# FNet mixing and a gelu MLP in one fp32 kernel: small products and a lane swap later in their step, and the next batch's first-stage groups in other steps

## The chip, the cores and the metric

The kernel runs on 1 core of one Trainium2 chip. The metric is the device time in microseconds (us), the median of several runs. Three runs of the kernel before took 1855.01, 1855.89 and 1854.38 us: median 1855.01 us.

## The reference

```python
def _attn_ref(x):                       # x: (8, 3008, 256) float32
    X = np.fft.fft(x, axis=1)
    X = np.fft.fft(X, axis=2)
    return X.real.astype(np.float32)

def _moe_ref(x, w_in, w_out):           # (24064, 256), (256, 2048), (2048, 256), float32
    h = x @ w_in
    g = h * (1.0 / (1.0 + np.exp(-1.702 * h)))
    return (g @ w_out).astype(np.float32)

def reference(x, moe_w_in, moe_w_out):  # the real part of the 2-d transform, then the MLP
    a = _attn_ref(x)
    return _moe_ref(a.reshape(8 * 3008, 256), moe_w_in, moe_w_out)
```

## The kernel before

**Work.** A transform over 3008 = 47 x 64 points is done in two stages per batch: `fold1` (GpSimd) adds and subtracts mirrored rows of the input tile `xt` in place, `mix1` (TensorE, 47-row products) is the first stage, `spill` and `fill` carry its result through DRAM into the tile `t4`, `rotate` mends one column, and `stage2` (TensorE, products on 64 rows and 32 columns) is the second stage, whose result `pq` is already folded over the model dimension. The first matrix of the MLP has the last transform folded into it (`wcs`), so the hidden layer is `wcs` times `pq`; its second half comes from the first by symmetry (`backward` subtracts the hidden value from twice its even part, reversed in order). The second matrix product is done by a Strassen-like scheme: 7 large products of which the kernel keeps 3 (`product`), and whose other 4 are split again into 7 small ones each (`small_products`, key k = 1 to 7).

**Steps.** The hidden layer is walked in 384 steps: 8 batches of 48 steps, each batch 3 blocks of 16, each block two halves (`hh`) of NP = 8 steps. This document writes t for the number of a step and m for t modulo 48. Steps with m = 8 to 15 are 226 wide, all others 256. Eight steps that share one output are a group; it ends where m is 7, 15, 23, 31, 39 or 47. In the trace, batch 2 (t = 96 to 143) runs from 495.31 to 720.15 us.

**What a step t issues**, in the order of the loop from line 989, from t = 8 on:

- TensorE: `begin(t, 1)` (second half of the hidden values, 8 records `x<-pq,wcs`), then `product` of step t-3 (LAG = 3; 12 records `o<-big,wo`), `begin(t+1)` (8 records), and the small products. Those of an odd step t' come in two parts: `one` = (1, 2, 4, 7) in step t'+3, which is even, and `other` = (5, 6, 3) in step t'+4, which is odd. One k is 8 records of 128 columns. `cut` says how many of the three products of `product` stand ahead of `begin(t+1)`.
- ScalarE: `forward(t)` (L607, gelu out of PSUM), `doubled(t+1)` (L604, twice the even part), `activate_back(t)` (L614), `middle(t+2)` (two L592, which start the PSUM bank of step t+2).
- VectorE: `backward(t)` (L565), `sums(t-1)` in even steps (L629, L630), `deeper` (three L651 in odd steps, one in even steps).
- GpSimd: `sums(t)` (L622, L623).

Each engine works its own list in order. The hidden values of a step lie in PSUM bank b0 or b1, by the parity of t. `middle(t+2)` can write that bank only when `backward(t)` has read it, `begin(t+2)` adds to what `middle(t+2)` wrote, and `begin(t+1, 1)` may go on only when `doubled(t+1)` has copied the even part out.

**The end of a group** with last step g: ScalarE copies out of PSUM in step g+3 (`combine`, L754 and L756), VectorE adds the small results in step g+4 (`combine_small`, four L786), ScalarE exchanges lanes in step g+5 (`swap`, three copies L794 to L796), VectorE adds again in step g+5 (`combine_last`, L768 and L804), and turns and stores the two halves in steps g+6 and g+7 (`turn_last`, L737).

**The next batch beside it.** A table `extra` says at the end of which step a piece of the next batch is issued. For batch 0 the folds run in steps 11 to 26 and `mix1` in 16, 20, 25, 28; for batches 1 to 6 the folds run at m = 6 to 21 and `mix1` at m = 12, 15, 19, 23. `stage2` stands at m = 8, 24 and 40. A step that holds `mix1` or `stage2` is called special: these take the step's own bank (b0 or b1) and b2 for their result, so `middle(t+2)` is put off into the next step, ahead of its `forward`. The step after a special one is called `after`: there `cut` is 3, and one k of the small products stands ahead of `begin(t+1)`. The folds issue per part: part 0 is L225 and L227, part 1 is L230 and L231; the first part of a batch has L218, L219 and L220 ahead of it.

Of the kernel before, what the change touches and what calls it, by code (L numbers as in the profile page):

```python
# [43 lines left out]
LAG = 3  # L44
# [68 lines left out]
def kernel(ctx: ExitStack, tc, x, w_in, w_out, tab1, tab2, out):  # L113
    nc = tc.nc
# [470 lines left out]
    def middle(t):  # L585

        b, blk, hh, p = steps[t]
        n = width(t)
        x = xb[t] = bank("x", f"b{t % 2}")
        for i in range(2):  # L590
            f = 2 * p + i
            nc.scalar.activation(x[:, i * 256:i * 256 + n], nbt[b, blk][:, hh * 256:hh * 256 + n], ACTF.Copy,  # L592
                                 scale=af1[:, f:f + 1])
# [194 lines left out]
    def swap(t):  # L788

        if not group_end(t):  # L790
            return
        n = width(t)
        one, two_, kept = (free(big[lo:lo + 64], RES + at, [512, 2], [1, n]) for lo, at in ((64, 0), (0, 256), (64, 1024)))
        nc.scalar.copy(kept, two_)  # L794
        nc.scalar.copy(two_, one)
        nc.scalar.copy(one, kept)  # L796
# [136 lines left out]
    def at(t, fn, *args):  # L933
        extra.setdefault(t, []).append((fn, args))
# [22 lines left out]
        at(7 + i, small_weights, i)  # L957
    for b in range(B):
        t0 = b * NBLK * NF
        late = 0 if b else 5  # L960
        if b + 2 < B:
            for k in range(3):
                at(t0 + 11 + k, paced, t0 + 11 + k)
                at(t0 + 11 + k, turn, b + 2, k)
        if b + 1 < B:
            for c in range(NCH):
                for part in range(2):
                    at(t0 + 6 + 2 * c + part + late, fold1, b + 1, c, part, nc.gpsimd)
                if c % 2:
                    k = t0 + 9 + 2 * c + late + (c == (5 if late else 1))  # L970
                    at(k, mix1, b + 1, c // 2)
                    for half in range(2):
                        at(k + 1, spill, b + 1, half, c // 2)
            for blk in range(NBLK):
                at(t0 + 27 + blk + late, paced, t0 + 27 + blk + late)
                at(t0 + 27 + blk + late, fill, b + 1, 4 * blk, 4 * blk + 4)
            if b + 2 < B:
                for k in range(4):
                    at(t0 + 31 + 2 * k + late, paced, t0 + 31 + 2 * k + late)
                    at(t0 + 31 + 2 * k + late, load_x, b + 2, k)  # L980
            at(t0 + 36 + 3 * (late > 0), rotate, b + 1)
        for blk in range(NBLK):
            nxt = (b, blk + 1) if blk + 1 < NBLK else (b + 1, 0)
            if nxt[0] < B:
                at(t0 + blk * NF + 8, stage2, *nxt)
                at(t0 + blk * NF + 9, nyquist_out, *nxt)
                at(t0 + blk * NF + 10, nyquist, *nxt)

    for t in range(n + LAG):
        if t < NP:  # L990
            if t == NP - 3:
                spare[:] = [tag for tag in spare if tag[0] == "o"] + ["b2"]
            if t == NP - 1:
                middle(NP)
            hidden(t)
            if t == NP - 1:
                begin(NP)
                no_row(1024)
            if t == 0:
                squares(in2, nc.scalar)  # L1000
                nyquist(0, 0)
                low_up(in2)
                low_down(in2)
            if t in rows_at:
                first_row(rows_at[t])
            if t >= LAG and t != LAG + 1:
                product(t - LAG, 0, None)
            if t == LAG:
                product(1, 0, None)
            if t == 5:  # L1010
                bounds(("out", 2))
            if t == 6:
                low_down(("out", 3))
            if t:
                activate(t - 1)
            if t == 3:
                bounds(("in", 3))
            if t == 5:
                bounds(("out", 3), False)
            if t in early:  # L1020
                fold_w(early[t])
            rows(t)
            if t == NP - 1:
                doubled(NP)
                middle(NP + 1)
        else:
            after, special = (any(fn in (mix1, stage2) for fn, _ in extra.get(k, ())) for k in (t - 1, t))
            if t < n:
                begin(t, 1)
            if t == NP:  # L1030
                activate(t - 1)
            if after and t + 1 < n:
                middle(t + 1)
            if t < n:
                forward(t)
            while waiting:
                m, ps = waiting.pop()
                mixed(m, 1, ps)
            opening = (t - LAG) % NP == 0 and t >= NP + LAG
            one, other = (t - LAG, (1, 2, 4, 7)), (t - LAG - 1, (5, 6, 3))  # L1040
            if opening:
                small_products(*other)
            cut = 0 if opening and not after else 3 if after else 2
            product(t - LAG, 0, cut)
            if after:
                small_products(one[0], one[1][:1])
                small_products(other[0], () if opening else other[1][:1])
            if t + 1 < n:
                begin(t + 1)
            if not opening:  # L1050
                small_products(other[0], other[1][after:])
            product(t - LAG, cut, 6 if t - LAG == last else None)
            small_products(one[0], one[1][after:])
            swap(t - LAG - 2)
            if t < n:
                backward(t)
            if t + 1 < n:
                doubled(t + 1)
            if t < n:
                activate_back(t)  # L1060
                sums(t, nc.gpsimd)
            if t + 2 < n and not special:
                middle(t + 2)
            combine_small(t - LAG - 1)
            if t - LAG == last:
                product(last, 6, None)
            sums(t - 1, nc.vector)
            deeper(t - 2, 0)
            deeper(t - 3, 1)
        if t == NP:  # L1070
            psu.close()
            low = ctx.enter_context(tc.tile_pool(name="low", bufs=1, space=PS))
            pot["low"] = low.tile([128, 3 * 512], F32, tag="low", name="low")
        if t >= LAG:
            combine(t - LAG)
            combine_last(t - LAG - 2)
            turn_last(t - LAG - 3, 0)
            turn_last(t - LAG - 4, 1)
        if t >= NP:
            spare[:] = [f"b{t % 2}"] * special + ["b2"]  # L1080
        for fn, args in extra.get(t, ()):
            fn(*args)
# [28 lines left out]
```

## Time and profile before

| | |
|---|---|
| median of the runs | 1855.01 us |
| the profiled execution | 1854.86 us |
| its span | 1853.1 us |
| TensorE busy | 1836.6 us (99%) |
| VectorE busy | 1520.9 us (82%) |
| ScalarE busy | 1150.5 us (62%) |
| GpSimd busy | 975.2 us (53%) |
| one batch (t = 96 to 143) | 224.84 us |

In the rows of the timeline a group of records of one kind has the start of its first record and the time to the end of its last. TensorE's matmuls overlap, so what counts there is the time from one start to the next: 8 records of 256 columns take 0.86 to 0.87 us from start to start, 8 of 128 columns 0.43 to 0.44 us.

### The profile page before, as it was taken

How to read it: one execution, taken by the hardware profiler on the slowest of the kernel's cores; microseconds unless marked ns; L12 is line 12 of the kernel's file. 1: busy time of each engine (PE TensorE's matmuls, PEld its weight loads, DVE VectorE, ACT ScalarE, POOL GpSimd, SP SyncE). 2: the span in 40 equal slices, each digit the busy share in tenths (PEclk: the TensorE clock that was granted, in tenths of full speed). 3: DMA queues.
4: the chain of work that ended last, by engine and by line, in shares of the span. 5: the costliest groups of instructions: out<-in, count | busy, mean ns of one | idle time of the engine just before them, and what ended most of it. 6: DMA issues, size and time to landing. Idle time of an engine off the chain costs nothing.

```text
span 1853.1 us, 56093 instructions
## 1 busy us (share of the span) xinstructions
PE 1836.6 (99%) x23722; PEld 1401.3 (76%) x23722; DVE 1520.9 (82%) x2222; ACT 1150.5 (62%) x2241; POOL 975.2 (53%) x1053
## 2 busy tenths in 40 slices
PE   8999999999999999999999999999999999999998
PEld 4677777777777777777777777777777777778776
DVE  6988778887798778987789878888888888878874
ACT  5666656665666666666566666666665666656663
POOL 4776446744368434773348643485445754444442
PEclk9999999999999999999999999999999999999999
DMA  8721340215012240223302132121411111100111
GB/s 280 181 61 34 85 67 19 72 52 99 19 46 48 73 81 13 52 50 90 57 13 67 43 86 52 19 75 35 103 31 23 37 46 36 31 19 13 23 19 24
DMA packets 149707, 105.31 MB, mean 57 GB/s; under 512 B 106057, under 2 KB 130665, under 8 KB 148896
## 3 DMA queue, kind: packets, MB, share of 16 engines
q1 hardware_dynamic: 146624, 99.68, 23.6%
q8 instruction: 187, 3.06, 0.7%
q10 hardware_dynamic: 2832, 2.05, 0.5%
q14 instruction: 64, 0.52, 0.1%
HBM read 64.41 MB, written 48.05 MB: 61 GB/s over the span
## 4 chain that ended last, share of the span: by engine, by line
PE 80%; DVE 9%; POOL 4%; ACT 2%; DMA 2%; issue 2%; SPq 0%; DVEq 0%; ACTq 0%; POOLq 0%
PE x L184 29%; PE o L184 22%; PE low L685 21%; PE o L685 3%; DVE big L651 3%; PE ps L255 2%; DVE big L786 2%; DVE big L565 1%; PE ps L365 1%; POOL xt L227 1%; DVE big L629 1%; POOL big L623 1%; DMA xt<-in_x_dram 1%; ACT big L607 1%; DMA Td<-big 1%
## 5 line engine op out<-in xcount | busy, mean ns | idle before, releaser
L622 POOL TENSOR_TENSOR big<-big 128x256 f32<-128x256 f32 (+1 forms) x376 | 353.0, 939 | 825.1 <-ACT big L614 691.4
L184 PE MATMUL x<-pq,wcs 128*64 128x256 f32 (+1 forms) x6016 | 768.8, 376 | 2.0 <-ACT g L604 1.4
L651 DVE TENSOR_TENSOR big<-big 128x512 f32<-128x512 f32 (+1 forms) x736 | 623.1, 861 | 23.4 <-PE low L685 4.7
L184 PE MATMUL o<-big,wo 128*64 128x256 f32 (+1 forms) x4800 | 620.8, 375 | 0.1
L184 PEld LDWEIGHTS x<-pq,wcs 128*64 128x64 f32 x6016 | 412.3, 137 | 186.0 <-issue 15.0
L184 PEld LDWEIGHTS o<-big,wo 128*64 128x64 f32 x4800 | 341.6, 137 | 148.0 <-DVE big L629 0.5
L604 ACT ACTIVATE g<-x 128x512 f32<-128x512 f32 (+1 forms) x376 | 221.6, 589 | 366.3 <-PE x L184 365.0
L565 DVE TENSOR_TENSOR big<-g,x 128x512 f32<-128x512 f32 (+2 forms) x440 | 254.1, 589 | 209.4 <-ACT big L607 209.0
L592 ACT ACTIVATE x<-nb,af 128x256 f32<-128x256 f32 (+1 forms) x752 | 352.9, 469 | 79.7 <-DVE pq L371 63.6
L685 PE MATMUL low<-big 128*64 128x128 f32 (+1 forms) x5888 | 382.8, 270 | 0.0
L685 PEld LDWEIGHTS low<-big 128*64 128x64 f32 x5888 | 337.5, 137 | 29.2
L623 POOL TENSOR_TENSOR big<-big 128x256 f32<-128x256 f32 (+1 forms) x376 | 352.6, 938 | 0.0
L607 ACT ACTIVATE big<-x 128x512 f32<-128x512 f32 (+1 forms) x376 | 219.2, 583 | 127.5 <-PE x L184 121.3
L614 ACT ACTIVATE big<-big 128x512 f32<-128x512 f32 (+1 forms) x376 | 231.9, 617 | 46.0 <-DVE big L565 44.0
L685 PE MATMUL low<-big,wo 128*64 128x128 f32 (+1 forms) x2944 | 220.4, 271 | 0.1
L685 PEld LDWEIGHTS low<-big,wo 128*64 128x64 f32 x2944 | 171.3, 137 | 4.2 <-DVE big L651 1.4
L630 DVE TENSOR_TENSOR big<-big 128x512 f32<-128x512 f32 (+1 forms) x188 | 160.8, 855 | 6.5
L629 DVE TENSOR_TENSOR big<-big 128x512 f32<-128x512 f32 (+1 forms) x188 | 137.3, 730 | 5.3 <-POOL big L622 5.3
L786 DVE TENSOR_TENSOR big<-big,low 128x512 f32<-128x512 f32 (+3 forms) x184 | 109.0, 609 | 3.5
L685 PEld LDWEIGHTS o<-big,wo 128*64 128x64 f32 x1472 | 92.2, 137 | 25.0
L685 PE MATMUL o<-big,wo 128*64 128x128 f32 (+1 forms) x1472 | 110.0, 270 | 0.0
L227 POOL TENSOR_TENSOR xt<-xt 111x510 f32<-111x510 f32 x56 | 86.0, 1535 | 4.4
(95 smaller groups left out, 966.2 us busy)
## 6 DMA issues: line engine op xcount, KB each, us to landing
out_dram<-os SPq DMA_DIRECT2D x284, 64.0 KB
t<-Td SPq DMA_DIRECT2D x22, 512.0 KB
Td<-xt SPq DMA_DIRECT2D x56, 192.0 KB
xt<-in_x_dram SPq DMA_DIRECT2D x14, 512.0 KB
xt<-Xr SPq DMA_DIRECT2D x14, 512.0 KB
nb<-Nd SPq DMA_DIRECT2D x23, 256.0 KB
out_dram<-os SPq DMA_DIRECT2D x96, 56.0 KB
Xr<-in_x_dram SPq DMA_DIRECT2D x7, 752.0 KB
```

Source lines behind the costliest of these rows:

```text
L184: nc.tensor.matmul(out[c0:c0 + 64], lhsT=lhs[:, c0:c0 + 64], rhs=rhs, skip_group_check=True, **how)
L565: nc.vector.tensor_tensor(free(out, at + m - 1, [by, 2], [RUN, blocks], [-1, m]), *ins, op=op)
L592: nc.scalar.activation(x[:, i * 256:i * 256 + n], nbt[b, blk][:, hh * 256:hh * 256 + n], ACTF.Copy, scale=af1[:, f:f + 1])
L604: nc.scalar.activation(two(g[:], n), two(xb[t][:], n), ACTF.Copy, scale=2.0)
L607: nc.scalar.activation(front(t), two(xb[t][:], width(t)), ACTF.Gelu_apprx_sigmoid)
L614: nc.scalar.activation(back(t), back(t), ACTF.Gelu_apprx_sigmoid)
L622: eng.tensor_tensor(right(t, S1, n), left(t, A21, n), right(t, A22, n), op=ALU.add)
L623: eng.tensor_tensor(left(t, S3, n), left(t, A11, n), left(t, A21, n), op=ALU.subtract)
L629: eng.tensor_tensor(s2, s1, a11, op=ALU.subtract)
L630: eng.tensor_tensor(s4, a12, s2, op=ALU.subtract)
L651: nc.vector.tensor_tensor(out, i0, i1, op=how)
L685: nc.tensor.matmul(o, lhsT=lhs, rhs=rhs, start=first_in, stop=(p == NP - 2), skip_group_check=True)
```

## The change

Four things change.

1. In a step after a special one no small products stand ahead of `begin(t+1)` any more: all of `other` follows `begin(t+1)`, as it does in every other step, and all of `one` ends the step. `cut` stays 3 there.
2. `swap` is issued after `middle(t+2)`, at the end of the step's ScalarE work. Before, it was issued ahead of `doubled(t+1)`.
3. `combine_last` and both `turn_last` come one step later (g+6, g+7, g+8).
4. For batches 1 to 6 the folds run from the last step of the batch before to m = 14 (7 steps earlier), `mix1` at m = 6, 14, 16, 22, `fill` at m = 25 to 27, `load_x` at 29, 31, 33, 35 and `rotate` at 31. For batch 0 the folds stay, `mix1` is at 16, 22, 23, 30, `fill` at 33 to 35, `load_x` at 34, 36, 38, 40, `rotate` at 39.

```diff
-        late = 0 if b else 5
+        folds, mixes, fills = (-1, (6, 14, 16, 22), 25) if b else (11, (16, 22, 23, 30), 33)
...
-                    at(t0 + 6 + 2 * c + part + late, fold1, b + 1, c, part, nc.gpsimd)
+                    at(t0 + folds + 2 * c + part, fold1, b + 1, c, part, nc.gpsimd)
                 if c % 2:
-                    k = t0 + 9 + 2 * c + late + (c == (5 if late else 1))
+                    k = t0 + mixes[c // 2]
                     at(k, mix1, b + 1, c // 2)
...
-                at(t0 + 27 + blk + late, fill, b + 1, 4 * blk, 4 * blk + 4)
+                at(t0 + fills + blk, fill, b + 1, 4 * blk, 4 * blk + 4)
...
-                    at(t0 + 31 + 2 * k + late, load_x, b + 2, k)
-            at(t0 + 36 + 3 * (late > 0), rotate, b + 1)
+                    at(t0 + fills + 4 + 2 * k - 3 * (b == 0), load_x, b + 2, k)
+            at(t0 + fills + 6, rotate, b + 1)
...
             product(t - LAG, 0, cut)
-            if after:
-                small_products(one[0], one[1][:1])
-                small_products(other[0], () if opening else other[1][:1])
             if t + 1 < n:
                 begin(t + 1)
             if not opening:
-                small_products(other[0], other[1][after:])
+                small_products(*other)
             product(t - LAG, cut, 6 if t - LAG == last else None)
-            small_products(one[0], one[1][after:])
-            swap(t - LAG - 2)
+            small_products(*one)
             if t < n:
                 backward(t)
...
             if t + 2 < n and not special:
                 middle(t + 2)
+            swap(t - LAG - 2)
             combine_small(t - LAG - 1)
...
             combine(t - LAG)
-            combine_last(t - LAG - 2)
-            turn_last(t - LAG - 3, 0)
-            turn_last(t - LAG - 4, 1)
+            combine_last(t - LAG - 3)
+            turn_last(t - LAG - 4, 0)
+            turn_last(t - LAG - 5, 1)
```

More of the change, by code (lines that the diff above doesn't have):

```diff
@@ L974 @@
             for blk in range(NBLK):
-                at(t0 + 27 + blk + late, paced, t0 + 27 + blk + late)
-                at(t0 + 27 + blk + late, fill, b + 1, 4 * blk, 4 * blk + 4)
+                at(t0 + fills + blk, paced, t0 + fills + blk)
+                at(t0 + fills + blk, fill, b + 1, 4 * blk, 4 * blk + 4)
             if b + 2 < B:
                 for k in range(4):
-                    at(t0 + 31 + 2 * k + late, paced, t0 + 31 + 2 * k + late)
-                    at(t0 + 31 + 2 * k + late, load_x, b + 2, k)
-            at(t0 + 36 + 3 * (late > 0), rotate, b + 1)
+                    at(t0 + fills + 4 + 2 * k - 3 * (b == 0), paced, t0 + fills + 4 + 2 * k - 3 * (b == 0))
+                    at(t0 + fills + 4 + 2 * k - 3 * (b == 0), load_x, b + 2, k)
+            at(t0 + fills + 6, rotate, b + 1)
         for blk in range(NBLK):
```

## The prediction

> **What bounds the kernel now.** I read the page's first part, the waits, and then the timeline of batch 2 (t = 96 to 143, 495.31 to 720.15 us), each engine by itself.
>
> ```profile
> PE 1836.6 (99%) x23722; PEld 1401.3 (76%) x23722; DVE 1520.9 (82%) x2222; ACT 1150.5 (62%) x2241; POOL 975.2 (53%) x1053
> ```
>
> TensorE is the bound and its amount of work is the same after the change: the order is another, no product is added. So only its hand-overs can change. They are found from start to start: 16 records of 128 columns hand over after 0.87 us, 16 of 113 columns after 0.77, and a switch to `mix1` costs 0.10 more, in the new places too. In batch 2 I find these losses beyond that.
>
> Step m = 12 (t = 108), `mix1` waits for VectorE, which reads the bank late:
>
> ```profile
> 553.79 0.94 PE L685 MATMUL low<-big 128*64 128x113 f32 x16
> 554.42 0.68 DVE L565 TENSOR_TENSOR big<-g,x 128x448 f32<-128x448 f32 x2
> 555.24 0.29 PE L255 MATMUL ps<-e,w 47*64 47x129 f32 x1 [0.51 <-DVE big L565]
> ```
>
> Due at 553.79 + 0.77 + 0.10 = 554.66, started at 555.24: 0.57 us with rounding.
>
> Step m = 20 (t = 116), `swap` stands ahead of `doubled` (L604) after a special step:
>
> ```profile
> 591.04 0.57 ACT L794 COPY big<-big 64x452 f32<-64x452 f32 x1
> 591.64 0.57 ACT L795 COPY big<-big 64x452 f32<-64x452 f32 x1
> 592.25 0.57 ACT L796 COPY big<-big 64x452 f32<-64x452 f32 x1
> 592.84 0.60 ACT L604 ACTIVATE g<-x 128x512 f32<-128x512 f32 x1
> ...
> 592.21 1.04 PE L685 MATMUL low<-big 128*64 128x128 f32 x16
> 593.49 1.08 PE L184 MATMUL x<-pq,wcs 128*64 128x256 f32 x8 [0.23 <-ACT g L604]
> ```
>
> Due at 593.08, started at 593.49: 0.41, and 0.05 more, since each interrupted row takes 0.05 longer to its second pair. The same reading elsewhere gives 0.18 at m = 11 (a small product waits for L651), 0.16 at m = 13, 0.11 each at m = 25 and 41 (`doubled` late, as only two k stand between `begin(t+1)` and `begin(t+1, 1)`), 0.05 at m = 9. Sum: 0.57 + 0.46 + 0.18 + 0.16 + 0.22 + 0.05 = **1.64 us a batch**. For batches 1 to 6 that is 9.8 us; batch 0 has about 2.4, of which 1.5 in places that the change touches.
>
> **The change, part by part.**
>
> *No small products ahead of `begin(t+1)` in `after` steps.* Three k now cover `doubled`, 1.31 us instead of 0.87: the losses at m = 25 and 41 (0.11 or less) go, and that at 9. What it uncovers is `middle(t+1)`: after `stage2` in step 24 of batch 1 L592 ended at 391.25 us and `begin` started at 391.90; without 0.43 of small products it starts at 391.47, still 0.22 later. I take a gain of 0.27 a batch (nothing to 0.27), which is part of the 1.64.
>
> *Swap last on ScalarE.* The loss at m = 20 goes (0.46). But now three copies (515.27 to 517.19 in the row below, 1.92 us) stand between `middle(t+2)` and the next step's `forward` and `doubled`. The ordinary end of a group before, step m = 4 (t = 100, from 513.51 to 518.28; the next to 522.61):
>
> ```profile
> 515.27 0.62 ACT L794 COPY big<-big 64x512 f32<-64x512 f32 x1
> ...
> 516.57 0.62 ACT L796 COPY big<-big 64x512 f32<-64x512 f32 x1
> ...
> 518.37 0.97 ACT L592 ACTIVATE x<-nb,af 128x256 f32<-128x256 f32 x2
> 519.42 0.60 ACT L607 ACTIVATE big<-x 128x512 f32<-128x512 f32 x1
> 521.15 0.60 ACT L604 ACTIVATE g<-x 128x512 f32<-128x512 f32 x1 [1.13 <-PE x L184]
> ```
>
> Call x the end of L565 (`backward`) after the step's start; here 517.42, x = 3.91. The new chain is x + 0.05 + L614 0.62 + L592 0.97 + swap 1.92 + L607 0.60 + L604 0.60 + 0.10 to TensorE = x + 4.86, against 4.77 + 4.33 = 9.10 when `begin(t+2, 1)` is due. A wait of x - 4.24 follows: at x = 3.91 a slack of 0.33, at more a stall. So groups with no fold beside them (m = 21, 29, 37, 45) lose nothing.
>
> *Folds 7 steps earlier.* They run at m = 47 and 0 to 14 and now lie beside the ends at m = 2 to 6 and 10 to 14; before, beside 10 to 14 and 18 to 22. Beside folds VectorE's adds with both inputs in SBUF stretch:
>
> ```profile
> 136.82 3.48 DVE L651 TENSOR_TENSOR big<-big 128x512 f32<-128x512 f32 x3
> 140.22 0.67 DVE L565 TENSOR_TENSOR big<-g,x 128x512 f32<-128x512 f32 x1
> ...
> 138.16 1.58 POOL L227 TENSOR_TENSOR xt<-xt 111x510 f32<-111x510 f32 x1
> ...
> 544.99 2.30 DVE L630 TENSOR_TENSOR big<-big 128x452 f32<-128x452 f32 x1
> ```
>
> The first three rows are batch 0, step 19 to 20 (from 135.88): three L651 took 3.48 us instead of the 2.07 of three at 0.69, and x became 5.02. The new steps 3 and 4 have the same fold part (L225, L227) in the same phase. L630, 0.69 alone, took 2.30 while four GpSimd adds passed.
>
> The Trainium skill ("SBUF — State Buffer", Who interferes with whom) says that a VectorE instruction with two SBUF inputs contends with a GpSimd one that reads SBUF, and the second to issue waits until the first is done. The 2.30 us row is harsher: it let several pass. By the page's one wait each stretch would be at most one L227 (1.27 us uncontended), and the sum below would sit near its lower half.
>
> Per batch 1 to 6, low, high and taken:
>
> - Step 5, `begin(6, 1)` behind swap: x between 3.91 (no fold) and 5.02 (batch 0): 0 to 0.9, with 0.05 and a late `begin(6)`. Taken 0.5, the middle: the phase is batch 0's, but step 3 starts its sums some 0.4 earlier.
> - Step 6, `mix1` waits for L565. `forward(5)` behind swap ends near 3.3 in step 5, L565 at 4.0, then L651 x3 (2.4), L768, L804 (0.7 + 1.0 uncontended) and L565 0.7: 4.0 + 2.4 + 1.7 + 0.7 = 8.8, or 4.5 in step 6, and 0.4 of contention as in the row of L768 (1.21): 4.9 against 4.77. Low 0.2; high 1.25, if L804 has to let an L227 of 1.27 by. Taken 0.7.
> - Step 13, 226 wide: x was 4.75 at m = 12 before (555.10 - 550.35). The chain with its rows (0.58, 0.93, 1.92, 0.55, 0.55, 0.15) is x + 4.68 against 4.21 + 3.84 = 8.05: a wait of x - 3.37. The 1.3 us of `mix1` that stood at the end of step 12, in which VectorE and ScalarE caught up, are gone. x from 3.7 (L630 not stretched) to 4.85: 0.3 to 1.5. Taken 1.0.
> - Step 14, `mix1` behind the same L768 and L804 of step 13: 0.35 to 1.7 by the same two cases. Taken 0.8.
>
> New: 3.0 taken, from 0.85 to 5.35. Old: 1.64, all gone (m = 11 may keep its 0.18, which is inside the range). Net +1.4 a batch, x 6 = +8.2 (from -4.7 to +22.3).
>
> *Batch 0*: swap behind x = 5.02 stalls step 21 by 0.8, `mix1` at 22 as in step 6 by 0.7, and of the 1.5 there before 0.5 may stay: +0.5 (-1.5 to +2). *Batch 7*: no folds, `stage2` twice: -0.15. *One step later for L768, L804, L737*: counted in the steps above; at the end of the run nothing: the last such group's L737 falls in step 383, before the last outputs are summed.
>
> *SP's queue.* `fill`, `load_x` and their pacing transfers move ahead of the stores of groups 31 and 23; the page's L345 transfers 512 KB. Before, the third `fill` of batch 2 was issued at 642.11 us, behind stores, and `rotate` came five steps later. After, it is issued near step 27 and `rotate` stands in 31, four steps or 18 us. DMA was 0.25 busy over batch 2 (the windows): hidden, cost 0. If a fill came late, TensorE would stop at the end of step 31 for the rest.
>
> Sum: 8.2 + 0.5 - 0.15 = +8.5 on the profiled execution's 1854.86 (span 1853.1 and 1.8 around it), 0.15 under the median of 1855.01: **1863 us**.
>
> **Rivals.**
>
> 1. *The waits go and nothing takes their place (faster).* GpSimd's L227 never gets between L651 and L565 in step 3, so x stays at 3.91. For it: in step 3 the last L651 issued at 516.13 without a fold, about when L225 would leave the port, and L227 follows L225 only 0.08 later. Against: 2.30 us rows in two steps of every batch. It decides at x = 4.24 in step 5 and 3.5 in step 13. With the low ends, -4.7 - 1.5 = 1849; with all losses gone 1844.
> 2. *An even trade.* Only step 13 (1.0) and step 14 or 6 (0.7) stall: 1.7 against 1.64, 1855.
> 3. *VectorE loses the port at each of the four places.* 5.35 a batch: 1855 + 22.3 + 2 = 1879.
> 4. *`rotate` waits for `fill`.* Late by half a step of 4.5 us, 2.3 x 7 = +16 on the sum, 1879. The 18 us of room and a DMA share of 0.25 speak against it.
>
> **How the numbers follow.** A change of 0.2% (3.7 us) is about what can be told from none. Forecast (1859 to 1872): 0.45. Rivals 3 and 4: 0.17. Rival 2 (1851.3 to 1858.7): 0.11. Rival 1: 0.27. So faster 0.27, same 0.11, slower 0.62. The range leaves out about 0.1 of the lowest and 0.06 of the highest: 1848 to 1880; the forecast's own is 1859 to 1872.
>
> **What would show it.** Right: in the new rows `mix1` at m = 6 and 14 starts late behind L565; at m = 6 and 14 the step's first `x<-pq,wcs` waits for L604, with L794 to L796 ahead of L607; m = 21, 25 and 41 without a loss; L651 or L804 of over 1.3 us beside L227 in steps 3 to 6. Wrong: x in step 4 at 3.9 and in step 12 under 3.5, or L565 of steps 6 and 14 done before the small products are.

## The result, and the profile after

The kernel after takes **1865.59 us** (median of 6 runs, 1865.06 to 1868.7); the kernel before took 1855.3 us beside it (6 runs, 1854.38 to 1858.23). The ratio is 1.0058, with a 95% interval of 1.0045 to 1.0071: the change makes the kernel slower by 10.3 us. The prediction was 1863, with a range of 1848 to 1880. The profiled execution of after took 1865.06 us, its span is 1863.3.

The first line of the page of after, with busy time, share of the span and instructions of each engine:

```profile
PE 1839.8 (99%) x23722; PEld 1401.0 (75%) x23722; DVE 1533.8 (82%) x2222; ACT 1151.9 (62%) x2241; POOL 1013.2 (54%) x1053
```

Every engine has as many instructions as before. What grew most are the times of VectorE (+12.9 us) and GpSimd (+38.0), without any new work: their instructions last longer beside each other, as the rows below show.

The waits of before, then those of after (engine, line, what it waited for: us in total, times, longest):

```profile
ACT big L614 <- DVE big L565: 44.0, 70, 1.2
...
PEld x L184 <- ACT x L592: 8.6, 33, 0.7
...
PEld x L184 <- ACT g L604: 4.0, 12, 0.5
```

```profile
ACT big L614 <- DVE big L565: 116.1, 160, 1.7
...
PEld x L184 <- ACT x L592: 17.0, 38, 0.8
...
PEld x L184 <- ACT g L604: 9.8, 14, 0.8
```

Most of the story is in these three lines: ScalarE waits more for VectorE's `backward` (L565), and TensorE more for the two things that ScalarE makes behind it, the start of the next bank (L592) and the doubled copy (L604). What is not in them is `mix1`, which waits for L565 itself.

Where in a batch is it? Batch 2 runs from 496.55 to 722.96 us, so it is 226.41 us long, 1.57 more than before. First VectorE's rows in the kernel before, where no fold lies beside step 4 (from 513.51 us):

```profile
511.57 2.46 DVE L786 TENSOR_TENSOR big<-big,low 128x512 f32<-128x512 f32 x4
513.95 2.88 DVE L651 TENSOR_TENSOR big<-big 128x512 f32<-128x512 f32 x3
516.74 0.68 DVE L565 TENSOR_TENSOR big<-g,x 128x512 f32<-128x512 f32 x1
```

Then the timeline of after, from the last L651 of step 2 to step 6 (steps 4 to 6 start at 514.80, 519.57 and 524.47 us):

```profile
509.65 2.45 DVE L651 TENSOR_TENSOR big<-big 128x512 f32<-128x512 f32 x1
...
513.47 2.46 DVE L786 TENSOR_TENSOR big<-big,low 128x512 f32<-128x512 f32 x4
515.84 3.39 DVE L651 TENSOR_TENSOR big<-big 128x512 f32<-128x512 f32 x3
517.09 1.59 POOL L227 TENSOR_TENSOR xt<-xt 111x510 f32<-111x510 f32 x1
519.15 0.68 DVE L565 TENSOR_TENSOR big<-g,x 128x512 f32<-128x512 f32 x1
520.40 0.97 ACT L592 ACTIVATE x<-nb,af 128x256 f32<-128x256 f32 x2
522.69 0.62 ACT L796 COPY big<-big 64x512 f32<-64x512 f32 x1
523.33 0.60 ACT L607 ACTIVATE big<-x 128x512 f32<-128x512 f32 x1
523.83 0.59 ACT L604 ACTIVATE g<-x 128x512 f32<-128x512 f32 x1
524.47 1.08 PE L184 MATMUL x<-pq,wcs 128*64 128x256 f32 x8 [0.22 <-ACT g L604]
...
528.17 0.96 DVE L804 TENSOR_TENSOR big<-big 128x768 f32<-128x768 f32 x1
528.28 1.97 POOL L227 TENSOR_TENSOR xt<-xt 111x510 f32<-111x510 f32 x1
529.05 0.68 DVE L565 TENSOR_TENSOR big<-g,x 128x512 f32<-128x512 f32 x1
529.78 0.32 PE L255 MATMUL ps<-e,w 47*64 47x129 f32 x1 [0.27 <-DVE big L565]
```

Read it from the top. The L651 of step 2 takes 2.45 us beside an L227 and the L622 behind it, where it took 0.68 before (at 508.12). So the four L786 begin 1.33 us ahead of step 4, where it was 1.94 before. Then the three L651 take 3.39 us instead of 2.88; the last of them, from 517.58, takes 1.65 instead of 0.69, beside L227. So L565 of step 4 ends at 519.83, which is x = 5.03 us after the step's start, where it was 3.91 before. Of these 1.12 us, 0.6 come out of step 2 and 0.5 from the three L651. ScalarE then does L614, L592, the three copies of `swap` (the last is L796), `forward` and `doubled` in a row, and TensorE's `begin(6, 1)` starts at 524.47; the wait on the row is that of the records, from start to start it is 0.39, and 0.13 more for `begin(6)` in the same step. In step 6 VectorE has L768 and L804 ahead of L565, and `mix1` (L255) starts right behind it, 0.34 late. Steps 12 to 14 (from 554.21, 558.43 and 563.43 us) are the same story, narrower and dearer:

```profile
558.30 0.68 DVE L565 TENSOR_TENSOR big<-g,x 128x448 f32<-128x448 f32 x2
...
560.48 0.98 PE L184 MATMUL x<-pq,wcs 128*64 128x226 f32 x8 [0.30 <-ACT x L592]
...
563.43 0.98 PE L184 MATMUL x<-pq,wcs 128*64 128x226 f32 x8 [0.42 <-ACT g L604]
...
568.56 1.09 PE L255 MATMUL ps<-xt,w 47*64 47x256 f32 x16 [0.50 <-DVE big L565]
```

x is 4.77 here. From start to start `begin(14)` is 0.47 late, `begin(14, 1)` 0.59, `begin(15)` 0.15 and `mix1` 0.57. On the other side, the losses of before at m = 11, 12, 20, 25 and 41 are gone: step 25 takes 4.38 us from start to start, where it took 4.44, and step 20 4.77, where it took 5.22.

The sum over the profiled executions: batches 1 to 6 together are 10.1 us longer (1358.83 against 1348.70), batch 0 from t = 8 on 0.2, batch 7 0.3, and step 8 is reached 0.5 earlier, together the 10.2 us between 1854.86 and 1865.06.

### The profile page after: what moved, and what is told of

It is laid out like the page before. It is cut to its first block, busy times and chain, and to the rows that moved or that the text cites. A ratio compares the mean times of both kernels' runs of the same rounds, so it can differ in the third digit from the quotient of the medians.

```text
span 1863.3 us, 56073 instructions
## 1 busy us (share of the span) xinstructions
PE 1839.8 (99%) x23722; PEld 1401.0 (75%) x23722; DVE 1533.8 (82%) x2222; ACT 1151.9 (62%) x2241; POOL 1013.2 (54%) x1053
## 4 chain that ended last, share of the span: by engine, by line
PE 77%; DVE 15%; ACT 4%; issue 2%; DMA 2%; POOL 0%; DVEq 0%; ACTq 0%; SPq 0%; POOLq 0%
PE x L184 29%; PE o L184 21%; PE low L685 20%; DVE big L651 5%; PE o L685 3%; DVE big L565 3%; DVE big L786 2%; PE ps L255 2%; PE ps L365 1%; DVE big L629 1%; ACT big L607 1%; ACT x L592 1%; DVE big L768 1%; DMA xt<-in_x_dram 1%; DVE big L804 1%
## 5 line engine op out<-in xcount | busy, mean ns | idle before, releaser
L622 POOL TENSOR_TENSOR big<-big 128x256 f32<-128x256 f32 (+1 forms) x376 | 372.5, 991 | 798.3 <-ACT big L614 666.9
L651 DVE TENSOR_TENSOR big<-big 128x512 f32<-128x512 f32 (+1 forms) x736 | 638.7, 884 | 20.5 <-PE low L685 3.0
L604 ACT ACTIVATE g<-x 128x512 f32<-128x512 f32 (+1 forms) x376 | 221.7, 590 | 351.1 <-PE x L184 350.8
L565 DVE TENSOR_TENSOR big<-g,x 128x512 f32<-128x512 f32 (+2 forms) x440 | 254.7, 590 | 217.9 <-ACT big L607 217.8
L592 ACT ACTIVATE x<-nb,af 128x256 f32<-128x256 f32 (+1 forms) x752 | 352.6, 469 | 83.9 <-DVE pq L371 64.5
L685 PE MATMUL low<-big 128*64 128x128 f32 (+1 forms) x5888 | 377.6, 270 | 0.0
L623 POOL TENSOR_TENSOR big<-big 128x256 f32<-128x256 f32 (+1 forms) x376 | 374.0, 995 | 0.0
L614 ACT ACTIVATE big<-big 128x512 f32<-128x512 f32 (+1 forms) x376 | 232.2, 617 | 116.3 <-DVE big L565 116.1
L607 ACT ACTIVATE big<-x 128x512 f32<-128x512 f32 (+1 forms) x376 | 219.9, 585 | 82.8 <-PE x L184 69.5
L630 DVE TENSOR_TENSOR big<-big 128x512 f32<-128x512 f32 (+1 forms) x188 | 144.9, 771 | 6.5
L629 DVE TENSOR_TENSOR big<-big 128x512 f32<-128x512 f32 (+1 forms) x188 | 147.2, 783 | 1.6 <-POOL big L622 1.6
L786 DVE TENSOR_TENSOR big<-big,low 128x512 f32<-128x512 f32 (+3 forms) x184 | 109.0, 609 | 3.4
L227 POOL TENSOR_TENSOR xt<-xt 111x510 f32<-111x510 f32 x56 | 90.4, 1615 | 4.4
```

Source lines behind the costliest of these rows:

```text
L565: nc.vector.tensor_tensor(free(out, at + m - 1, [by, 2], [RUN, blocks], [-1, m]), *ins, op=op)
L604: nc.scalar.activation(two(g[:], n), two(xb[t][:], n), ACTF.Copy, scale=2.0)
L607: nc.scalar.activation(front(t), two(xb[t][:], width(t)), ACTF.Gelu_apprx_sigmoid)
L614: nc.scalar.activation(back(t), back(t), ACTF.Gelu_apprx_sigmoid)
L622: eng.tensor_tensor(right(t, S1, n), left(t, A21, n), right(t, A22, n), op=ALU.add)
L623: eng.tensor_tensor(left(t, S3, n), left(t, A11, n), left(t, A21, n), op=ALU.subtract)
```

## The experiments

All kernels are compared with the kernel before on the same chip; "waits" are TensorE's in batch 2, from start to start beyond what is due, as in the prediction. Where a length of a batch is given, it is the mean of batches 1 to 5 in the profile; before it is 224.77, after 226.40.

### Each part alone

**The small products behind `begin(t+1)`, alone.**

```diff
-            if after:
-                small_products(one[0], one[1][:1])
-                small_products(other[0], () if opening else other[1][:1])
...
-                small_products(other[0], other[1][after:])
+                small_products(*other)
...
-            small_products(one[0], one[1][after:])
+            small_products(*one)
```

> The kernel before with the first part of the change alone: no small products ahead of begin(t+1) in the step after a special one; swap, combine_last and the places of folds and mix1 as before. Theory (the loss comes from swap at the end of ScalarE's list together with folds beside a group's end): a small gain, the waits at m = 25 and 41 and 13 go (0.38 us a batch), 1853 us. Rival (the small products had covered middle, and begin(t+1) now waits for L592 after every special step): 0.2 us at each of 7 steps a batch, 1855 + 8 = 1863 us.

Measured: 1851.16 us, ratio 0.9977 (0.9967 to 0.9986), a gain of 4.2 us. It is larger than the 0.27 a batch of the prediction: the batch is 224.07. m = 25 and 41 give their 0.11 each and m = 13 its 0.16, but m = 11 gives its 0.18 too, and at m = 12 the wait of `mix1` for L565 (0.57) is gone. Against that `begin(10)` in step 9 now waits 0.24 for L592. The gains at m = 11 and 12 and this wait were not in the working; the run of one small product further down shows what ties them together.

**`swap` at the end of the step, alone**, with `combine_last` and `turn_last` one step later as in the change.

```diff
-            swap(t - LAG - 2)
             if t < n:
                 backward(t)
...
                 middle(t + 2)
+            swap(t - LAG - 2)
...
-            combine_last(t - LAG - 2)
-            turn_last(t - LAG - 3, 0)
-            turn_last(t - LAG - 4, 1)
+            combine_last(t - LAG - 3)
+            turn_last(t - LAG - 4, 0)
+            turn_last(t - LAG - 5, 1)
```

> The kernel before with the second part alone: swap behind middle(t+2), combine_last and turn_last one step later. Theory: with mix1 still at the end of step 12 the late backward is covered, so no new wait there; the wait at m = 20 (0.46 us a batch) goes: 1852.5 us. Rival (swap at the end of ScalarE's list is a loss by itself, whatever lies beside it): every group's end stalls the next step by some 0.5 us, 6 a batch, 1855 + 20 = 1875 us.

Measured: 1868.67 us, ratio 1.0072 (1.0055 to 1.0089): a loss of 13.3, and the theory missed. The wait at m = 20 goes as expected (0.40), but m = 9 loses 0.83, m = 13 0.18 (its 0.11 of before stays), m = 15 0.46, m = 23 0.19. Steps 9 and 13 stand behind `stage2` and `mix1`, steps 15 and 23 hold a `mix1`. It is not what the rival said either: behind the swaps of m = 4, 28, 36 and 44 nothing waits. At m = 9, rows of the timeline of this kernel:

```profile
538.32 1.20 DVE L629 TENSOR_TENSOR big<-big 128x512 f32<-128x512 f32 x1 [0.94 <-POOL big L622]
...
541.71 1.43 DVE L371 STREAM_TRANSPOSE pq<-ps 128x256 f32<-128x256 f32 x4
...
543.58 0.98 PE L184 MATMUL x<-pq,wcs 128*64 128x226 f32 x8 [0.66 <-ACT x L592]
```

`stage2`'s first product ran at 539.12. Its transposes L371 start 2.59 us later, behind L629, L630 and L651; in the kernel before they start 1.55 later (536.28 to 537.83). L592, which needs the transposed result, follows them. VectorE is not busy all that time: it idles for 0.94 us ahead of L629, until GpSimd's L622 (from 537.55) is done. GpSimd had worked without a break since the L622 of step 6, the first fold parts among it, and that L622 came behind an L614 that waited for L565 of step 6 (from 529.47). In front of that L565 now stand L768 and L804 (527.34 to 529.55). So by the rows what costs at m = 9 is the second half of this part, the end of a group one step later, and through the folds; no run takes the two halves apart.

**The new places, alone.**

```diff
-        late = 0 if b else 5
+        folds, mixes, fills = (-1, (6, 14, 16, 22), 25) if b else (11, (16, 22, 23, 30), 33)
...
-                    at(t0 + 6 + 2 * c + part + late, fold1, b + 1, c, part, nc.gpsimd)
+                    at(t0 + folds + 2 * c + part, fold1, b + 1, c, part, nc.gpsimd)
...
-                    k = t0 + 9 + 2 * c + late + (c == (5 if late else 1))
+                    k = t0 + mixes[c // 2]
```

(and `fill`, `load_x` and `rotate` as in the change)

> The kernel before with the third part alone: folds from m = -1, mix1 at m = 6, 14, 16, 22 (batch 0: 16, 22, 23, 30). Theory: backward in step 4 still ends near 5.0 us and in step 12 near 4.7, but doubled is no longer behind swap, so the wait of 0.45 us at the start of step 6 and of 0.6 at the start of step 14 are not there; begin(t+2) behind L592 still waits 0.2 in step 5 and 0.5 in step 13, mix1 in step 6 and 14 a little: 1853 to 1857 us. Rival (the places alone make the loss): as the whole change, 1865 us.

Measured: 1878.51 us, ratio 1.0125 (1.011 to 1.014), a loss of 23.2, far outside both expectations. In batch 2 TensorE waits 0.77 at m = 6, 0.63 at m = 9, 0.77 at m = 11, 0.47 at m = 13 and 1.40 at m = 14. x of step 4 is 3.91 here and not near 5.0 as expected, with the folds in the same steps as in after; the run with two parts below shows why. This is the dearest part, and the other two take 12.9 of it back.

### Two parts at a time

**Small products and swap**, the first two diffs above together, in the old places:

```diff
-                small_products(other[0], other[1][after:])
+                small_products(*other)
...
-            swap(t - LAG - 2)
...
+            swap(t - LAG - 2)
...
-            combine_last(t - LAG - 2)
+            combine_last(t - LAG - 3)
```

> The first two parts together with the old places of folds and mix1. Theory: both small gains add up, 0.4 + 0.46 us a batch: 1850 to 1851 us, faster than both kernels. Rival (swap and products are the loss): 1860 us or more.

Measured: 1861.42 us, ratio 1.0033 (1.002 to 1.0046), the rival's side. m = 9 waits 1.27, somewhat more than the 0.24 of the one part and the 0.83 of the other together; m = 13 0.53, m = 15 0.24.

**Small products and places**, swap and the ends of the groups as before; this is the change with its second and third parts undone:

```diff
+            swap(t - LAG - 2)
             if t < n:
                 backward(t)
...
-            swap(t - LAG - 2)
...
-            combine_last(t - LAG - 3)
-            turn_last(t - LAG - 4, 0)
-            turn_last(t - LAG - 5, 1)
+            combine_last(t - LAG - 2)
+            turn_last(t - LAG - 3, 0)
+            turn_last(t - LAG - 4, 1)
```

> The whole change with swap, combine_last and turn_last put back where they were (products and places alone). Theory A (swap at the end of ScalarE's list is what the late backward is paid through): the waits behind doubled at the start of steps 6 and 14 (0.39 and 0.59 us in batch 2 of the changed kernel) are not there: 1865.6 - 1.1 x 6 = 1858 us. Theory B (the folds beside two group ends are the cause, and the order of swap only moves the wait from doubled to middle and mix1, as the run with the places alone suggests): no faster than the whole change, 1866 us or more.

Measured: 1868.93 us, ratio 1.0071 (1.0054 to 1.0088). Theory B holds. Undoing the late swap doesn't help, it costs another 3.3 us; the intervals of the two ratios overlap, but in the profiles batches 1 to 6 together are 3.6 us longer than those of after, and each of them is. Without it TensorE waits at m = 6 (0.77), 9 (0.95), 13 (0.47) and 14 (1.40). Rows of step 5 to 6 of this kernel:

```profile
525.91 1.29 DVE L804 TENSOR_TENSOR big<-big 128x768 f32<-128x768 f32 x1
...
529.40 1.08 PE L184 MATMUL x<-pq,wcs 128*64 128x256 f32 x8 [0.60 <-ACT x L592]
```

L768 and L804 come one step earlier here, in front of the L565 of step 5 (from 527.13), and TensorE waits for the L592 behind it instead of for L604 or `mix1`. L565 of step 4 is not late, x is 3.91: the L651 of step 2 takes 1.22 us and not 2.45, the four L786 begin 1.86 us ahead of step 4 (515.95) and not 1.33, and the last L651 is over (521.13) when L227 has hardly begun (520.55). So the steps in which the folds run don't fix x by themselves; by these rows some 0.5 us of phase decides which instruction meets which. The delay comes up one step later and is paid at another door.

**Swap and places**, the change with its first part undone:

```diff
+            if after:
+                small_products(one[0], one[1][:1])
+                small_products(other[0], () if opening else other[1][:1])
...
-                small_products(*other)
+                small_products(other[0], other[1][after:])
...
-            small_products(*one)
+            small_products(one[0], one[1][after:])
```

> The late swap and the new places with the small products as before (the change without its first part). If the first part saves beside the late swap what it saved beside the old one in the new places (1878.5 to 1868.9, 9.6 us): 1875 us. If its saving was bound to the swap standing ahead of doubled in steps 6 and 14, which the late swap takes away: within 3 us of the kernel after, 1863 to 1869 us.

Measured: 1874.32 us, ratio 1.0104 (1.0089 to 1.0119). The first expectation holds: beside the new places the small products are worth 8.7 us with the late swap and 9.6 without it. The waits that they take away are those of m = 11 (0.77, a small product that waits for L651), 15 and 17 (0.15 each).

All eight combinations, in us:

| | old places | new places |
|---|---|---|
| nothing else | 1855.3 | 1878.5 |
| small products behind | 1851.2 | 1868.9 |
| swap and group ends later | 1868.7 | 1874.3 |
| both | 1861.4 | 1865.6 |

The small products always gain (4.1 to 9.6). The late swap costs 10 to 13 in the old places and gains 3 to 4 in the new ones. The new places cost 23 and 18 with the early swap, 6 and 4 with the late one. So no part has a price of its own; the two that move VectorE's work decide together.

### Is it the folds?

Both kernels without the add L227, the largest of the fold's four (111 x 510). The sum of the mirrored rows is left out, so less is computed.

```diff
-            low = free(t, at + 1, [D, 2], [1, D - 1])
-            eng.tensor_tensor(low, low, free(t, up + D - 1, [-D, 2], [-1, D - 1]), op=ALU.add)
```

> The changed kernel without the add L227 of the folds (the sum of mirrored rows is left out, 8 adds a batch; the result is not the transform). Theory (VectorE's adds wait for the port behind this long GpSimd add): backward of step 4 ends near 3.9 us instead of 5.0, the waits of steps 5, 6, 13 and 14 shrink from 2.9 us a batch to under 1: 1852 us or less. Rival (any GpSimd work beside the end of a group does it, or the order on ScalarE): 1862 us or more.

> The kernel before without L227 (the same left out), as the measure for the run above. Theory: the waits of m = 11 and 12 shrink, those at 20, 25 and 41 stay: 1850 to 1853 us, so that the change costs little or nothing without L227. Rival: the difference between the two kernels stays at 10 us.

After without L227: 1849.46 us, ratio 0.9966 (0.9954 to 0.9978). Before without L227: 1855.03 us, ratio 0.9995 (0.9985 to 1.0006). In the old places L227 costs nothing; in the new ones it costs 16.1 us. Without it the change would be a gain of 5.6. x falls to 3.92 and 3.66. The waits at m = 5 and 13 are gone but for 0.06 at m = 13, those of `mix1` at m = 6 and of `begin(10)` at m = 9 too; that of `mix1` at m = 14 (0.57) and 0.15 for `begin(15)` stay. For the kernel before, the theory was wrong in that the waits of m = 11 and 12 would shrink: they stay at 0.15 and 0.58, and L630 at m = 10 takes 2.30 us there without L227 too, beside L231, L622 and L623.

**The folds one step earlier**, so that L225 and L227 fall in even steps and L230 and L231 in odd ones, which asks whether it is this one add:

```diff
-        folds, mixes, fills = (-1, (6, 14, 16, 22), 25) if b else (11, (16, 22, 23, 30), 33)
+        folds, mixes, fills = (-2, (6, 14, 16, 22), 25) if b else (11, (16, 22, 23, 30), 33)
```

> The kernel after with its folds one step earlier still, from the last but one step of the batch before: L225 and L227 then run in even steps (2, 4, 10, 12), as they did in the kernel before, and L230 with L231 in the odd ones. Theory (L227 beside the three L651 of steps 3 and 11 and beside L768 and L804 of steps 5 and 13 is what makes L565 late): x of steps 4 and 12 falls from 5.03 and 4.77 to under 4.4 and 4.0, the waits of m = 5, 6, 13 and 14 shrink by more than half, 1851 to 1857 us. Rival (any fold beside a group's last sums costs the same, whichever of its adds it is): x stays over 4.7, 1862 us or more.

Measured: 1874.51 us, ratio 1.0109 (1.0094 to 1.0124); the rival's side. x of step 4 stays at 5.01; that of step 12 falls to 4.07, but `mix1` at m = 6 and 14 is later by 0.40 than in after, and m = 1 and 3 lose 0.33 and 1.14 that after doesn't have. Rows of step 4 of this kernel:

```profile
519.83 3.37 DVE L651 TENSOR_TENSOR big<-big 128x512 f32<-128x512 f32 x3
...
520.34 1.18 POOL L230 TENSOR_TENSOR xt<-xt 111x254 f32<-111x254 f32 x1
```

The three L651 take 3.37 us beside L230 and L231 (from 521.48), as they took 3.39 beside L225 and L227. So either fold part can stretch these L651, not the one add alone.

**The folds away from the ends of the groups.** The kernel after with nothing left out; only the steps of the 16 parts differ, and with them those of `mix1`, `fill`, `load_x` and `rotate`.

```diff
-        folds, mixes, fills = (-1, (6, 14, 16, 22), 25) if b else (11, (16, 22, 23, 30), 33)
+        folds, mixes, fills = ((-1, 0, 1, 2, 6, 7, 8, 9, 10, 14, 15, 16, 17, 18, 22, 23), (6, 14, 19, 26), 30) if b else (range(11, 27), (16, 22, 23, 30), 33)
...
-                    at(t0 + folds + 2 * c + part, fold1, b + 1, c, part, nc.gpsimd)
+                    at(t0 + folds[2 * c + part], fold1, b + 1, c, part, nc.gpsimd)
```

> The kernel after, nothing left out, with the 16 fold parts of batches 1 to 6 put where no group ends beside them: at the end of the batch before and at m = 0, 1, 2, 6 to 10, 14 to 18, 22 and 23, so none in 3 to 5, 11 to 13 and 19 to 21 (the steps of L786, of the three L651 behind it, and of L768 and L804); mix1 at 6, 14, 19 and 26, fill at 30 to 32, rotate at 36. Theory (what made x late is any large fold part beside the L651 that follow the four L786, and the waits of m = 5, 6 and 13 come of it; the late swap needs x under 4.24 and 3.5): x of steps 4 and 12 falls under 4.3 and 3.6, what is left is the 0.6 of mix1 at m = 14 that stayed without L227, and the time is that of the change without L227, 1848 to 1852 us. Rival (the folds stretch VectorE by about the same wherever they lie, and the late swap pays for it): 1858 us or more.

Measured: 1857.71 us, ratio 1.0015 (1.0005 to 1.0024), 7.9 less than after. By the time alone this lies nearly at the rival's limit; the rows tell why. x is 4.07 in step 4 and 3.66 in step 12 (just over the 3.6 of the theory), the waits of m = 5 and 9 are gone, that of `mix1` at m = 6 is 0.05 and that of m = 13 is 0.06, and at m = 14 0.15 for `begin(15)` and the 0.57 of `mix1` stay. So far it is nearly what the theory said. But a new wait of 0.93 stands at m = 27, rows of this kernel:

```profile
514.75 2.43 DVE L651 TENSOR_TENSOR big<-big 128x512 f32<-128x512 f32 x3
...
628.18 1.08 PE L184 MATMUL x<-pq,wcs 128*64 128x256 f32 x8 [0.76 <-ACT g L604]
```

The first row is step 4 again: 2.43 us for the three, a microsecond less than in after. The other is the price of the place chosen for `mix1`, m = 26: in the step after it, which is also the first step of a new group's `product`, all of `product` and of the small products stand ahead of `begin(28)`, so nothing is left between `begin(28)` and `begin(28, 1)` to cover `doubled`. Six times 0.93 is 5.6 us; without it the time would be some 1852 us, an estimate from the two numbers, not a run.

### What is better than both

**The small products behind, and the swap late only where it helped**, for the group whose swap falls in the step after a special one (m = 20); the others, and the folds, as before. The small products are moved as in the first run; the diff shows the rest.

```diff
-            swap(t - LAG - 2)
+            if not after:
+                swap(t - LAG - 2)
...
+            if after:
+                swap(t - LAG - 2)
...
-            combine_last(t - LAG - 2)
-            turn_last(t - LAG - 3, 0)
-            turn_last(t - LAG - 4, 1)
+            for later in range(2):
+                for k, done in enumerate((combine_last, lambda g: turn_last(g, 0), lambda g: turn_last(g, 1))):
+                    g = t - LAG - 2 - later - k
+                    if group_end(g) and later == any(fn in (mix1, stage2) for fn, _ in extra.get(g + LAG + 1, ())):
+                        done(g)
```

> The first part of the change (products) on the kernel before, and swap behind middle(t+2), with combine_last and turn_last one step later, only for a group whose swap falls into a step after a special one (m = 20 of batches 1 to 6). Theory: the 0.46 us wait at m = 20 goes and no other comes: 1851.2 - 0.41 x 6 = 1848.7 us. Rival (one step later for the last sums costs as much behind the mix1 of step 19): 1851 us or more.

Measured: **1849.72 us**, ratio 0.9971 (0.996 to 0.9983), 5.4 less than before, between the theory and the rival and nearer the theory. The waits that the late swap of every group brought to m = 9 (1.27), 13 and 15 are gone but for the 0.27 of the small products at m = 9, so it was the late swaps and ends of the other groups that cost there; this run doesn't say which of the two. The wait at m = 20 is gone as well. Against the small products alone (1851.16) it is 1.4 us, and the intervals of the two ratios overlap; in the profiles batches 1 to 6 together are 1.4 us shorter.

**One small product back ahead of `begin(t+1)`, in step m = 9 alone**, to save these 0.27:

```diff
+            ahead = t % 48 == 9
+            if ahead:
+                small_products(other[0], other[1][:1])
             if t + 1 < n:
                 begin(t + 1)
             if not opening:
-                small_products(*other)
+                small_products(other[0], other[1][ahead:])
```

> The kernel of the run with the small products behind and the swap late at m = 20 alone, with one small product put back ahead of begin(t+1) in the step m = 9 alone. Theory (what is left there is begin(10) waiting for L592, 0.27 us a batch): the wait at m = 9 goes, 0.3 x 7 = 2 us less, 1847.6 us. Rival (the small product ahead makes the wait of m = 11 for L651, 0.18, come back): within 0.7 us of 1849.7.

Measured: 1853.33 us, ratio 0.999 (0.998 to 1.0). The wait at m = 9 is gone, and those of m = 11 (0.14) and of `mix1` at m = 12 (0.58) are back: the rival's mechanism, and more. In the profiles batches 1 to 6 are 2.0 us longer together, batches 0 and 7 are equal to 0.02, and step 8 is reached 4.3 us later (84.80 against 80.47 us), in code that the edit doesn't touch. So of the 3.6 us between the medians only 2.0 are shown to come from the edit. How can saving 0.27 us on TensorE cost 0.7? Rows of m = 10 without the small product ahead:

```profile
544.26 1.04 DVE L630 TENSOR_TENSOR big<-big 128x452 f32<-128x452 f32 x1
...
545.00 0.82 POOL L622 TENSOR_TENSOR big<-big 128x226 f32<-128x226 f32 x1 [0.19 <-ACT big L614]
```

and with it:

```profile
549.23 2.29 DVE L630 TENSOR_TENSOR big<-big 128x452 f32<-128x452 f32 x1
...
549.74 0.66 POOL L622 TENSOR_TENSOR big<-big 128x226 f32<-128x226 f32 x1
```

Without it, step 9 ends later on TensorE, ScalarE's L614 comes later, and GpSimd idles for 0.19 us before L622. L630 gets in and takes 1.04. With it, GpSimd's adds follow each other without a break and L630 takes 2.29, as in the kernel before (2.30). The run of the small products alone has the 1.04 and the 0.19 too: this is where that part had its unexpected gain at m = 11 and 12.

The other batches bear this out but for one. In all kernels, where GpSimd idled for 0.18 us or more ahead of that L622, L630 of m = 10 took 1.06 us or less. Without a gap it took 2.28 to 2.84, except in batch 5 of the kernel before and of the run with the small product ahead: 1.04, without a gap. With the small products behind, alone or with the swap late at m = 20, it is batch 5 that lacks the gap and has the 2.29 (alone it is 224.75 us long there, the others are 223.9). So with a gap L630 got in every time, but it can get in without one, and what decides then isn't shown.

## Why the prediction was right

**The sum.** It took new waits of 3.0 us a batch against 1.64 that go, +1.4, for batches 1 to 6 +8.2; the profiles have +10.1. Batches 0 and 7, taken at +0.5 and -0.15, have +0.2 and +0.3. The total, +8.5 against +10.2, is short by about as much as batches 1 to 6 are. The range, 1848 to 1880, holds the time of the kernel before as well, so the time alone says little for the working; the rows have to.

**The places.** The waits stand in the four steps that it names. In batch 2:

| step | taken | measured | |
|---|---|---|---|
| 5, `begin(6, 1)` behind swap | 0.5 | 0.57 | of it 0.13 at `begin(6)`, 0.05 at an interrupted row |
| 6, `mix1` behind L565 | 0.7 | 0.44 | 0.34, and two interrupted rows |
| 13, swap, 226 wide | 1.0 | 1.16 | 0.47 at `begin(14)`, 0.59 at `begin(14, 1)`, two interrupted rows |
| 14, `mix1` behind L768 and L804 | 0.8 | 0.82 | 0.57, 0.15 at `begin(15)`, two interrupted rows |
| 9, `begin(10)` | 0 | 0.19 | 0.14 behind L592, one interrupted row |

**x.** It turned on x: 0.5 at step 5 means x = 4.74, 1.0 at step 13 means 4.37. Measured were 5.03 and 4.77, at the upper ends of the bounds, the one the x of batch 0 nearly to the hundredth. The 0.4 us by which step 3 was to start its sums earlier, the reason for taking the middle, did not come: the L786 begin 1.33 us ahead of step 4, as in batch 0 (1.34), because the L651 of step 2 already takes 2.45 us beside a fold. The prediction counts no stretch of step 2's sums. That the waits came out right all the same is in part luck, by an error the other way. The chain behind x was put at x + 4.86 and x + 4.68; it took 9.67 - 5.03 = 4.64 and 9.22 - 4.77 = 4.45. The durations of consecutive ScalarE rows overlap: L604 starts at 523.83, before L607 (523.33 + 0.60) is over. Some 0.1 at each of two hand-overs was counted twice (L614 to L592, L607 to L604).

**Step 6** was mis-sized the other way. The 0.7 allowed for L804 letting an L227 by. It was L227 that waited (1.97 us, against 1.27 alone), and L804 took its 0.96. The wait is what three L651, L768 and L804 amount to behind a late start, without that stretch.

**The first part, with nothing taken for the uncovered `middle(t+1)`.** This step failed: 0.22 us of slack was read behind step 24 of batch 1, which is 256 wide and where L371 starts 1.19 us after `stage2`'s first product; behind step 8 it starts 1.55 after. In step 9, which is 226 wide and stands behind `stage2` at m = 8, `begin(10)` waits: 0.24 with this part alone, 0.14 in after, 1.27 beside the late swap in the old places. The gain of the part was undersized as well: 0.27 taken, 0.7 a batch where it is made alone, as the order of VectorE and GpSimd at m = 10 changes with it. Of the old losses, the 0.57 and 0.18 at m = 12 and 11 were counted for six batches; in batch 5 of before L630 takes 1.04, x of step 12 is 4.07, and the batch is 0.5 us shorter (224.31).

**The swap.** The chain through the three copies is the way on which the wait of step 5 comes, and the prediction has it right. But that the late swap is what makes the loss, which that chain suggests, is wrong: with the early one the kernel is slower by 3.3 us. Nor is it a price that can be carried to other places of the folds: alone it costs 13.3, by waits at m = 9, 13, 15 and 23 that the prediction's list of steps didn't reach.

**The folds** are the cause, and this is shown: without L227 the change gains 5.6 us where it lost 10.3; with all the work done but no fold beside the ends of the groups, x falls to 4.07 and 3.66 and the waits of steps 5, 6, 9 and 13 all but vanish. It isn't L227 in itself: L230 and L231 in its place stretch the L651 as much. Nor is it the fold's step in itself: with the early swap the same folds leave x of step 4 at 3.91 and cost more, a step later. What those runs lose is not taken apart by a run without L227.

The Trainium skill ("SBUF — State Buffer", Who interferes with whom) has one of two contending instructions wait until the other is done. In step 4 of after that is what the rows show: the last L651 took 1.65, 0.96 more than alone, within the one L227 that it met (1.59). In step 2 of after it isn't: L651 took 2.45, while the rest of an L227 and a whole L622 went by. Nor at m = 10 of before: L630 took 2.30, and although it starts ahead of L622, L622 and L623 were done first. (Not four adds passed there, as the prediction reads it, but the rest of L231 and these two; the fourth, L225, took 0.60 against 0.21 alone, so by its length it waited for L630.) So one wait gives the right size for a part of the new delay only, and the wrong one for the old wait of `mix1` at m = 12. The prediction had said that by one wait each its sum would sit near the lower half; the new waits came to 3.2 us a batch, just above what was taken.

**The rivals.** Rival 1 needed x under 4.24 and 3.5; it was 5.03 and 4.77. Rival 2 needed two of the four steps to stay free; none did. Rival 3 needed VectorE to wait at each of the four places; L804 in step 6 did not, L227 waited for it. Rival 4: `rotate` in step 31 costs the 0.09 that it cost in step 36 before, and no `fill` was late. The groups with no fold (m = 21, 29, 37, 45) lose nothing, as said.

**What stays open**: the 0.57 of `mix1` at m = 14, which is there with and without folds beside it, was not taken apart by a run of its own; by the rows it is L768 and L804 in front of the L565 of a step that is 226 wide. What lets L630 in without a gap in two of the batches is open, and so is whether the late swap or the late ends cost the 13.3 us in the old places.

## What to carry to other kernels

Work on an idle engine is not free if it makes the instructions of an engine that others wait for last longer: place it by what the other engine has to do in those steps, here away from the steps in which a group's sums pile up, and not by where the idle engine has time. When a change has several parts that all shift one engine's work, measure each with and without the others: here the same part costs 13 us or gains 4, by what else was done. And between two rows of the trace the start of the second, not the sum of two durations, is the price of the first.

## What the runs showed that was not expected

- L630 of m = 10, a VectorE add of 0.63 us alone, mostly waits through several GpSimd adds if these come without a gap (2.29 us), and gets in with a gap of 0.19 us on GpSimd (1.04 us). So 0.27 us more waiting on TensorE can be worth 0.7 us less a few steps later. In two of the profiled batches it got in without a gap, so the gap isn't all that decides.
- The add L227 costs nothing in one place (1855.03 us without it against 1855.08 with it, on one chip) and 16 us seven steps earlier.
- Moving the folds by a single step (from the last step of the batch before to the last but one) cost 8.9 us more. By the rows an L630 of m = 2 to 3 takes 2.48 us there, beside L231, L622, L623 and L225.
